# A fused attention and two-MLP kernel: its third layer by seven block products in place of eight

## The chip, the core and the metric

The kernel runs on one NeuronCore of one Trainium2 chip. The metric is device time in microseconds; less is better. The engines are named as the profile names them: TensorE (PE, and PEld for its weight loads), VectorE (DVE), ScalarE (ACT), GpSimd (POOL) and SyncE (SP), which here only issues DMAs.

## The reference, cut to what matters

```python
def reference(**kwargs):
    ...
    attn_out = _attn_ref(**attn_kwargs)          # 8 batches, 576 tokens each, 8 heads of 64
    x = attn_out.transpose(0, 2, 1, 3).reshape(B * S, H * D)      # 4608 x 512
    x = _moe_ref(x=x, **moe_kwargs)              # layers 1 and 2: max of three products, then w_out
    return _moe2_ref(x=x, **moe2_kwargs)

def _moe2_ref(x, w_in, w_out):                   # x 4608 x 512, w_in 512 x 2048, w_out 2048 x 512
    h = x @ w_in                                 # layer 3
    g = np.maximum(h, 0.0) + np.log1p(np.exp(-np.abs(h)))         # softplus
    return (g @ w_out).astype(np.float32)        # layer 4
```

Weights come as 64-bit floats, and the kernel narrows them itself.

## The kernel before, in words

The first part of the program goes over the eight batches. For each it computes attention and layers 1 and 2, and writes the result, transposed (512 features by 4608 tokens), to a DRAM tensor `x2d`. In this part the kernel also narrows `w_in` and `w_out` and writes them to the DRAM tensors `wi32` and `wo32` (`narrow_ahead`).

The second part computes layers 3 and 4. It goes over nine chunks `c` of 512 tokens and, in each, over sixteen blocks `f` of 128 of the 2048 hidden features. Every large product is made of three float32r matmuls: each operand is split into a high part and a low part (`split`: ScalarE copies the high part, VectorE subtracts it from the source to get the low one), and high times high, high times low and low times high are summed in PSUM.

`layer3(c, f)` issues 12 matmuls (four blocks of 128 input features, three terms each), all with a 128x128 stationary block of `w_in` and 512 moving columns, the tokens of the chunk. ScalarE then takes softplus from PSUM into `t`, and `split_g` splits it. `layer4(c, f, tt)` uses the split softplus as the stationary operand and 512 columns of `w_out` as the moving one; for one `f` it issues 12 matmuls, three for each of the four token blocks `tt`, and adds into one of four PSUM banks `acc`. The loop over `seq` issues `layer3` three steps ahead of `layer4`. The split `w_in` (`wi_parts`) stays in SBUF for the whole second part. The tokens of the next chunk are loaded and split during the current one (`load_x2`). After a chunk's last `f`, `store` copies the banks out and writes them with 32-row DMAs.

The last batch (`n + 1 == B`) has room for preparing the second part: in ten slots (six of layer 1, four of layer 2) the code loads `wi32` blocks and the first chunk of `x2d`, and splits them. Tile pools of that preparation lie where the attention's pools lay, so some loads wait for attention's last readers.

The order of instructions on each engine comes from a scheduler that keeps the order in which code is written, unless an instruction is free to go earlier; `tc.issue_after` pins work behind an instruction. SyncE issues nearly all DMAs in order: one that waits holds back all that are behind it. Its transfers also share one queue.

## Time and profile before

| | |
|---|---|
| median of three runs | 1338.63 us (1335.36 to 1340.78) |
| profiled execution, time | 1338.1 us |
| profiled execution, span from first to last instruction | 1336.1 us |
| TensorE busy (matmuls) | 1299.5 us, 97% of the span |
| VectorE busy | 539.5 us, 40% |
| ScalarE busy | 443.5 us, 33% |
| first matmul of layer 3 | 534.4 us from the span's start |
| last matmul of layer 4 | starts at 1331.6 us |

Busy times are sums over one profiled execution, and the two parts of the program differ: read each part by itself. A matmul's recorded duration contains the filling and emptying of the array and overlaps the next one's, so the cost of one in a stream is the interval between starts, not its duration.

### The profile page before, as it was taken

What the parts mean: (1) busy time and instruction counts of PE and PEld (TensorE: products, weight loads), DVE (VectorE), ACT (ScalarE), POOL (GpSimd) and SP (SyncE); (2) the same over time, 40 slices, a digit from 0 to 9 for tenths busy, and PEclk for the clock granted to TensorE, in tenths of its full rate; (3) what the DMA queues carried; (4) which work ended last, traced back from release to release, by engine and by line L of the source; (5) the groups of instructions that cost most, each with busy time, mean ns of one, the idle gap of its engine ahead of it and who ended that gap; (6) DMA issues with size and microseconds to landing.
All of it is one profiled execution on the core that took longest, in us unless ns stands there. A gap on an engine that the chain in (4) does not pass through costs nothing.

```text
span 1336.1 us, 20625 instructions
## 1 busy us (share of the span) xinstructions
PE 1299.5 (97%) x8656; PEld 1098.0 (82%) x8656; DVE 539.5 (40%) x904; ACT 443.5 (33%) x758; POOL 0.7 (0%) x6
## 2 busy tenths in 40 slices
PE   4879999999999999999999999999999999999998
PEld 3769898898988899888888888888888888888887
DVE  4787778786878746512111121121111211211111
ACT  3544434444343435623222222232222222322221
POOL 0000000000000000000000000000000000000000
PEclk9899999999999999999999999999999999999999
DMA  9883677877677407401002011010010110100101
GB/s 279 205 207 100 164 202 183 205 204 204 180 209 204 122 36 223 152 0 46 18 3 62 1 32 32 0 52 13 15 49 0 32 32 1 26 6 1 32 0 32
DMA packets 61853, 119.12 MB, mean 89 GB/s; under 512 B 11072, under 2 KB 28736, under 8 KB 61760
## 3 DMA queue, kind: packets, MB, share of 16 engines
q1 hardware_dynamic: 55984, 106.66, 29.8%
q10 hardware_dynamic: 5776, 11.14, 2.5%
q8 instruction: 68, 1.11, 0.4%
q14 instruction: 25, 0.20, 0.1%
HBM read 90.51 MB, written 27.26 MB: 88 GB/s over the span
## 4 chain that ended last, share of the span: by engine, by line
PE 92%; DVE 4%; DMA 2%; issue 1%; SPq 1%; ACT 1%; DVEq 0%
PE ps L396 58%; PE acc L766 10%; PE acc L767 10%; PE acc L765 10%; PE ps_w L375 2%; DMA wraw<-in_moe_w_dram 1%; PE ps_s L247 1%; PE ps_e L286 1%; PE ps_v L306 1%; DMA vt<-in_v_dram 1%; DVE pwlo L108 0%; DVE wraw L89 0%; PE ps_k L199 0%; DVE vT L223 0%; DVE wsb L97 0%
## 5 line engine op out<-in xcount | busy, mean ns | idle before, releaser
L108 DVE TENSOR_TENSOR glo<-t,ghi 128x512 fp32r<-128x512 f32 x144 | 99.7, 692 | 620.5 <-ACT ghi L107 620.5
L749 ACT ACTIVATE t<-ps 128x512 f32<-128x512 f32 x144 | 86.4, 600 | 546.7 <-PE ps L396 546.2
L396 PE MATMUL ps<-x2hi,wilo 128*128 128x512 f32 x576 | 228.0, 396 | 0.0
L396 PE MATMUL ps<-x2lo,wihi 128*128 128x512 f32 x576 | 227.0, 394 | 0.0
L396 PE MATMUL ps<-x2hi,wihi 128*128 128x512 f32 x576 | 226.7, 394 | 0.0
L767 PE MATMUL acc<-w2hi,glo 128*128 128x512 f32 x576 | 225.9, 392 | 0.0
L766 PE MATMUL acc<-w2lo,ghi 128*128 128x512 f32 x576 | 225.7, 392 | 0.0
L765 PE MATMUL acc<-w2hi,ghi 128*128 128x512 f32 x576 | 224.4, 390 | 0.0
L396 PE MATMUL ps<-a2hi,pwhi 128*128 128x288 f32 x576 | 129.5, 307 | 2.5 <-ACT a2hi L107 1.3
L396 PEld LDWEIGHTS ps<-x2lo,wihi 128*128 128x128 f32 x576 | 108.1, 188 | 25.8
L396 PEld LDWEIGHTS ps<-x2hi,wilo 128*128 128x128 f32 x576 | 108.3, 188 | 25.1
L766 PEld LDWEIGHTS acc<-w2lo,ghi 128*128 128x128 f32 x576 | 108.1, 188 | 25.0
L765 PEld LDWEIGHTS acc<-w2hi,ghi 128*128 128x128 f32 x576 | 108.2, 188 | 24.8
L396 PEld LDWEIGHTS ps<-x2hi,wihi 128*128 128x128 f32 x576 | 108.2, 188 | 24.6
L767 PEld LDWEIGHTS acc<-w2hi,glo 128*128 128x128 f32 x576 | 108.1, 188 | 23.1
L396 PE MATMUL ps<-a2lo,pwhi 128*128 128x288 f32 x576 | 124.6, 298 | 0.7 <-DVE a2lo L108 0.7
L396 PE MATMUL ps<-a2hi,pwlo 128*128 128x288 f32 x576 | 124.7, 299 | 0.0
L396 PEld LDWEIGHTS ps<-a2hi,pwhi 128*128 128x128 f32 x576 | 93.4, 192 | 15.8 <-ACT m L419 5.9
L396 PEld LDWEIGHTS ps<-a2lo,pwhi 128*128 128x128 f32 x576 | 94.0, 191 | 0.9 <-DVE a2lo L108 0.9
L396 PEld LDWEIGHTS ps<-a2hi,pwlo 128*128 128x128 f32 x576 | 94.0, 191 | 0.0
L107 ACT ACTIVATE ghi<-t 128x512 fp32r<-128x512 f32 x144 | 90.9, 631 | 4.2
L421 DVE TENSOR_TENSOR m<-ps,m 128x576 f32<-128x576 f32 x96 | 72.3, 753 | 30.6 <-PE ps L396 28.3
(85 smaller groups left out, 1300.4 us busy)
## 6 DMA issues: line engine op xcount, KB each, us to landing
qraw<-in_q_dram SPq DMA_DIRECT2D x112, 140.0 KB
kraw<-in_k_dram SPq DMA_DIRECT2D x96, 140.0 KB
wraw<-in_moe_w_dram SPq DMA_DIRECT2D x18, 512.0 KB
x2d<-xs ACTq DMA_DIRECT2D x32, 288.0 KB
x2r<-x2d SPq DMA_DIRECT2D x36, 256.0 KB
out_dram<-o SPq DMA_DIRECT2D x136, 64.0 KB
raw<-in_moe_w_in_dram SPq DMA_DIRECT2D x16, 512.0 KB
raw<-in_moe_w_out_dram SPq DMA_DIRECT2D x16, 512.0 KB
```

The source lines that it names most:

```text
L107: nc.scalar.activation(out=hi, in_=src, func=AF.Copy)
L108: nc.vector.tensor_tensor(out=lo, in0=src, in1=hi.bitcast(F32), op=ALU.subtract)
L247: nc.tensor.matmul(ps[G][cols, hh, :HS], w[rows, cols], x[rows, g, hh * HS : hh * HS + HS], start=True, stop=True,)
L286: nc.tensor.transpose(ps[: 32 * TI, i // hi, (i % hi) * P : (i % hi) * P + P], e[:, i], ident,)
L306: nc.tensor.matmul(ps[32 * g : 32 * g + 32, G, :D], t[:, i, 32 * g : 32 * g + 32], vt[n][:, NG * g + G, i, :], start=(i == 0), stop=(i == ...
L375: nc.tensor.matmul(ps[cols, G, : units * P].rearrange("p (w x) -> p w x", w=units), ppT[n][rows, cols], wsb[rows, 4 * c : 4 * c + units, g ...
L396: nc.tensor.matmul(o, w, xx, start=first, stop=last)
L421: nc.vector.tensor_tensor(out=m, in0=ps[:, :, :HS], in1=ms[n, f], op=ALU.max)
L749: nc.scalar.activation(out=t, in_=ps, func=AF.Softplus)
L765: nc.tensor.matmul(ps, ghi[:, cols], whi, start=(f == 0), stop=False)
L766: nc.tensor.matmul(ps, ghi[:, cols], wlo, start=False, stop=False)
L767: nc.tensor.matmul(ps, glo[:, cols], whi, start=False, stop=(f == F2 - 1))
```

## The change

Layer 3 is computed in units `(c, j)`, one for a pair of feature blocks `j` and `j + 8`. The weights of a pair are seen as 2x2 blocks (two halves of the 512 input features, two feature blocks), the tokens as 2x2 blocks (two halves of the input features, two halves of 256 tokens). One level of Strassen's scheme (Winograd's form) takes seven block products in place of eight; each is six matmuls of 256 columns (two blocks of 128 input features, three terms). It needs four sums of weight blocks, four sums of token blocks, and additions of the products, which VectorE makes (`sums`, and four additions in `layer3`). ScalarE copies the first product out of PSUM.

Weight sums are made once for a pair (`make_pair`), split, written to a DRAM tensor `wic` (14,336 bytes in each of 128 partitions, 1.835 MB a pair) and read back for every later chunk into a ring of two SBUF buffers (`get_pair`): pairs 2, 3, 0 and 1 are made in the last batch, 4 to 7 in chunk 0. `w_in` no longer stays in SBUF. The four PSUM banks of layer 3 are single-buffered (`l3`, tags l30 to l33). `layer4` takes a pair at once and runs one step behind. `wi32` is stored by pairs, in pieces of 512 bytes.

```diff
+    BATCH_END = {
+        0: [("load", 2)],
+        1: [("load", 3)],
+        2: [("make", 2), ("loadx", 0)],
+        4: [("make", 3), ("load", 0)],
+        5: [("load", 1)],
+        6: [("make", 0), ("makex", 0)],
+        7: [("makex", 1), ("makex", 2)],
+        8: [("makex", 3)],
+        9: [("make", 1), ("load", 4), ("load", 5)],
+    }
...
+                    def make_pair(j):
+
+                        u = wus.pop(j)
+                        sums(
+                            u,
+                            (
+                                (4, 0, 3, ALU.add),
+                                (5, 4, 1, ALU.subtract),
+                                (6, 1, 0, ALU.subtract),
+                                (7, 2, 5, ALU.subtract),
+                            ),
+                        )
+                        t = ring.tile([P, 2, 7, 2, P], F32R, tag="ring", name="wc")
+                        split(u[:, 1:8], t[:, 0], t[:, 1])
+                        nc.sync.dma_start(
+                            out=wic[j], in_=t.rearrange("p h a k x -> p (h a k x)").bitcast(F32)
+                        )
+                        pairs[j] = t
...
+    def product(out, w, x, wi, xi):
+        terms = [
+            (w[:, a, wi, k], x[b][:, xi, k]) for k in range(2) for a, b in ((0, 0), (0, 1), (1, 0))
+        ]
+        for i, (l, r) in enumerate(terms):
+            nc.tensor.matmul(out, l, r, start=(i == 0), stop=(i == len(terms) - 1))
+
+    def layer3(c, j):
...
+        w, x = pairs.pop(j), x2[c]
+        pa, pb, pc, pd = (
+            l3.tile([P, 2, HC], F32, tag=f"l3{i}", name=f"ps_3{i}") for i in range(4)
+        )
+        product(pa[:, 0], w, x, 0, 0)
+        product(pb[:, 0], w, x, 1, 1)
+        product(pb[:, 1], w, x, 4, 4)
+        product(pc[:, 0], w, x, 3, 3)
+        product(pc[:, 1], w, x, 5, 5)
+        product(pd[:, 0], w, x, 6, 2)
+        product(pd[:, 1], w, x, 2, 6)
+        h = cp.tile([P, 7, HC], F32, tag="h", name="h")
+        add = nc.vector.tensor_tensor
+        nc.scalar.activation(out=h[:, 3], in_=pa[:, 0], func=AF.Copy)
+        add(out=h[:, 0:5:4], in0=h[:, 3:4].to_broadcast([P, 2, HC]), in1=pb, op=ALU.add)
+        add(out=h[:, 5:7], in0=h[:, 4:5].to_broadcast([P, 2, HC]), in1=pc, op=ALU.add)
+        add(out=h[:, 3], in0=h[:, 6], in1=pc[:, 0], op=ALU.add)
+        add(out=h[:, 1:3], in0=h[:, 5:7], in1=pd, op=ALU.add)
+        done = last_of(mybir.EngineType.DVE)
+        g = h[:, 0:4].rearrange("p a t -> p (a t)")
+        nc.scalar.activation(out=g, in_=g, func=AF.Softplus)
+        hi = gp.tile([P, 2, CH], F32R, tag="ghi", name="ghi")
+        lo = gp.tile([P, 2, CH], F32R, tag="glo", name="glo")
+        split(g, hi.rearrange("p a t -> p (a t)"), lo.rearrange("p a t -> p (a t)"))
...
+    def get_pair(c, j):
+        if c == 0 and j >= 4:
+            make_pair(j)
+            return
+        pairs[j] = ring.tile([P, 2, 7, 2, P], F32R, tag="ring", name="wc")
+        nc.sync.dma_start(
+            out=pairs[j].rearrange("p h a k x -> p (h a k x)").bitcast(F32), in_=wic[j]
+        )
+
+    seq = [(c, j) for c in range(NCH) for j in range(FP)]
...
+    for i in range(len(seq) + 1):
         if i < len(seq):
...
+            c, j = seq[i]
+            with tc.issue_after(layer3(c, j)):
...
+                if i + 2 < len(seq):
+                    get_pair(*seq[i + 2])
...
+                if c + 1 < NCH:
+                    if j == 1:
+                        load_x2(c + 1)
+                    if 3 <= j < 7:
+                        make_x2(c + 1, j - 3, x2p0 if c % 2 else x2p1)
+        if i >= 1:
+            layer4(*seq[i - 1])
```

On TensorE, one unit of the second part of the program stood so before; `ps_7470` is the PSUM tile of `layer3(c, f)`, and the first of the matmuls of `layer4` follow:

```order
L396 MATMUL ps_7470<-x2hi,wihi 128x512
L396 MATMUL ps_7470<-x2lo,wihi 128x512
L396 MATMUL ps_7470<-x2hi,wilo 128x512
...
L765 MATMUL acc_6957<-w2hi,ghi 128x512
L766 MATMUL acc_6957<-w2lo,ghi 128x512
L767 MATMUL acc_6957<-w2hi,glo 128x512
```

In the changed program a unit of TensorE stands so; `wc` is the ring buffer with a pair's seven split weight blocks, and ps_7320 to ps_7323 are the banks pa, pb, pc and pd:

```order
L799 MATMUL ps_7320<-x2hi,wc 128x256
L799 MATMUL ps_7320<-x2lo,wc 128x256
L799 MATMUL ps_7320<-x2hi,wc 128x256 x2
...
L799 MATMUL ps_7321<-x2hi,wc 128x256
...
L799 MATMUL ps_7322<-x2hi,wc 128x256
...
L799 MATMUL ps_7323<-x2hi,wc 128x256
...
L845 MATMUL acc_6977<-w2hi,ghi 128x512
L846 MATMUL acc_6977<-w2lo,ghi 128x512
L847 MATMUL acc_6977<-w2hi,glo 128x512
```

Per two feature blocks, 24 matmuls of 512 columns have become 42 of 256 in layer 3, and the 24 of layer 4 follow as one group of 512 columns each, as before.

On SyncE's queue, from the last narrowed block of `w_out` to the end of the first loads of the second part, before (`wi_x` and `x2r` are loads for splitting, `w_x` is a block of `w_out`):

```order
L685 DMA wi_x<-wi_62 128x512 x4
L702 DMA x2r<-x2d 128x512
L685 DMA wi_x<-wi_62 128x512
...
L685 DMA wi_x<-wi_62 128x512 x3
L727 DMA w_x<-wo_63 128x512
L702 DMA x2r<-x2d 128x512
L727 DMA w_x<-wo_63 128x512 x3
```

The same place of SyncE in the changed program; `wu` is a pair's four weight blocks before the sums, `xu` the tokens before theirs, `wic<-wc` the write of a made pair and `wc<-wic` its reading back:

```order
L697 DMA wu<-wi_62 128x1024 x2
L720 DMA wic<-wc 128x3584
L728 DMA xu<-x2d 128x2x256 x4
L697 DMA wu<-wi_62 128x1024
L785 DMA w_x<-wo_64 128x512 x3
L720 DMA wic<-wc 128x3584
...
L728 DMA xu<-x2d 128x2x256
L720 DMA wic<-wc 128x3584
L697 DMA wu<-wi_62 128x1024
L785 DMA w_x<-wo_64 128x512 x2
L870 DMA wc<-wic 128x3584
```

The third and fourth writes (pairs 0 and 1) and two loads of `w_x`, which wait for VectorE's splits of earlier `w_out` blocks, now stand ahead of the first reading back, that of pair 2 for unit (0, 2).

On VectorE, inside chunk 0 where most is added (unit (0, 4), after the additions of unit (0, 3)), where there were only `w2lo` and `glo` of 512 columns before:

```order
L822 TENSOR_TENSOR h<-h,ps_7218 128x2x256
L823 TENSOR_TENSOR h<-h,ps_7219 128x512
L824 TENSOR_TENSOR h<-h,ps_7219 128x256
L825 TENSOR_TENSOR h<-h,ps_7220 128x512
L111 TENSOR_TENSOR w2lo<-w_x,w2hi 128x512 x2
L704 TENSOR_TENSOR wu<-wu 128x256 x3
L111 TENSOR_TENSOR x2lo<-xu,x2hi 128x1536
L111 TENSOR_TENSOR glo<-h,ghi 128x1024
L704 TENSOR_TENSOR wu<-wu 128x256
L822 TENSOR_TENSOR h<-h,ps_7321 128x2x256
L111 TENSOR_TENSOR wc<-wu,wc 128x1792
```

VectorE's work of a unit has grown from two subtractions to the four additions at the top, a subtraction twice as long, and, in chunk 0, the sums and splits of a later pair and of the next chunk's tokens.

## Rows read from the trace of the kernel before

**Rows 1.** The page: busy time of engines, TensorE's granted clock, the chain of waits.

```profile
PE 1299.5 (97%) x8656; PEld 1098.0 (82%) x8656; DVE 539.5 (40%) x904; ACT 443.5 (33%) x758; POOL 0.7 (0%) x6
...
PEclk9899999999999999999999999999999999999999
...
PE 92%; DVE 4%; DMA 2%; issue 1%; SPq 1%; ACT 1%; DVEq 0%
```

**Rows 2.** Waits, all engines, 534.3 to 1332 us: first two and last row.

```profile
engine line waited for: us in total, times, longest us
DVE glo L108 <- ACT ghi L107: 620.5, 132, 4.8
ACT t L749 <- PE ps L396: 546.2, 131, 4.3
...
ACT o L774 <- DMA out_dram<-o: 2.5, 1, 2.5
```

**Rows 3.** By instruction: count, duration min/median/max in ns, first and last start in us.

```profile
L396 PEld LDWEIGHTS ps<-x2hi,wihi x576: 187/188/188, 534.3 to 1320.0; 128*128 128x128 f32 x192
L396 PE MATMUL ps<-x2hi,wihi x576: 387/392/400, 534.4 to 1320.2; 128*128 128x512 f32 x192
...
L767 PE MATMUL acc<-w2hi,glo x576: 388/391/398, 545.8 to 1331.6; 128*128 128x512 f32 x192
```

**Rows 4.** Timeline of TensorE over layer 2 of the last batch: first and last.

```profile
515.20 0.43 PE L396 MATMUL ps<-hhi,wo_hi 128*128 128x288 f32 x2
...
534.13 0.43 PE L396 MATMUL ps<-hhi,wo_lo 128*128 128x288 f32 x2
534.40 0.39 PE L396 MATMUL ps<-x2hi,wihi 128*128 128x512 f32 x1
```

**Rows 5.** Timeline of weight loads and matmuls after an idle moment of the loads.

```profile
499.94 0.30 PEld L396 LDWEIGHTS ps<-a2hi,pwhi 128*128 128x128 f32 x2 [0.84 <-issue]
499.94 0.53 PE L396 MATMUL ps<-a2hi,pwhi 128*128 128x288 f32 x2
...
500.31 0.42 PE L396 MATMUL ps<-a2lo,pwhi 128*128 128x288 f32 x2
```

**Rows 6.** Groups by shape on VectorE and ScalarE: busy us, mean ns | idle before.

```profile
L108 DVE TENSOR_TENSOR glo<-t,ghi 128x512 fp32r<-128x512 f32 x144 | 99.7, 692 | 620.5 <-ACT ghi L107 620.5
L421 DVE TENSOR_TENSOR m<-ps,m 128x576 f32<-128x576 f32 x96 | 72.3, 753 | 30.6 <-PE ps L396 28.3 <-ACT m L419 0.7
L108 DVE TENSOR_TENSOR pwlo<-ps_w,pwhi 128x256 fp32r<-128x256 f32 x16 | 6.7, 422 | 5.4 <-ACT pwhi L107 5.4
L107 ACT ACTIVATE ghi<-t 128x512 fp32r<-128x512 f32 x144 | 90.9, 631 | 4.2
L107 ACT ACTIVATE pwhi<-ps_w 128x512 fp32r<-128x512 f32 x64 | 38.1, 596 | 39.7 <-PE ps_w L375 20.3 <-DVE pwlo L108 19.5
L107 ACT ACTIVATE pwhi<-ps_w 128x256 fp32r<-128x256 f32 x16 | 6.1, 383 | 5.3 <-DVE pwlo L108 3.6 <-PE ps_w L375 1.7
```

**Rows 7.** Windows: busy us of each engine (instructions), granted clock, DMA share, GB/s.

```profile
core 0: us, PE busy (x) PEld busy (x) DVE busy (x) ACT busy (x) POOL busy (x), PEclk, DMA share, GB/s
480.00:534.00 54.00, 54.00 (x439) 50.43 (x438) 30.76 (x46) 25.69 (x44) 0.00 (x0) 1.00 0.44 142
508.00:536.00 28.00, 28.00 (x207) 27.71 (x206) 17.70 (x29) 16.73 (x30) 0.00 (x0) 1.00 0.89 284
327.00:330.00 3.00, 3.00 (x24) 3.00 (x23) 1.62 (x3) 0.71 (x2) 0.00 (x0) 1.00 0.93 360
631.00:639.00 8.00, 8.00 (x36) 6.52 (x35) 1.63 (x3) 1.54 (x3) 0.00 (x0) 1.00 0.51 131
700.00:800.00 100.00, 100.00 (x435) 81.30 (x434) 18.36 (x27) 26.58 (x44) 0.00 (x0) 1.00 0.11 32
```

**Rows 8.** Timeline of the last batch: VectorE's last results of layer 1; SyncE's loads.

```profile
503.50 0.76 DVE L421 TENSOR_TENSOR m<-ps,m 128x576 f32<-128x576 f32 x1 [0.24 <-PE ps L396]
...
518.50 0.75 DVE L108 TENSOR_TENSOR hlo<-m,hhi 128x576 fp32r<-128x576 f32 x1
...
462.65 45.94 SPq L685 DMA_DIRECT2D wi_x<-wi  x4
508.63 0.43 SPq L702 DMA_DIRECT2D x2r<-x2d  x1
```

206 lines of the change are left out of this document (99 added, 107 removed).

## The prediction

> **What bounds the kernel now.** I read the page first. TensorE is busy for 97% of the span, at the full granted clock in nearly every slice, and the chain of waits lies on it for 92% [rows 1]. So I asked next whether it ever waits in the part that is changed: the list of waits from 534.3 us on has no TensorE row at all; VectorE and ScalarE wait for each other and for TensorE [rows 2]. From there on the kernel is a stream of matmuls and nothing else, and its time is their number times the interval between starts. The first starts at 534.4, the last at 1331.6 us [rows 3], with 9 x 16 x 24 = 3456 between them: 797.2 / 3455 = 230.7 ns for one of 512 columns. Layer 3 owns half of them, 1728 x 0.2307 = 398.7 us; layer 4's half is not touched. The other engines have room: in 700 to 800 us VectorE is busy for 18 and ScalarE for 27 of 100 us, and DMA moves 32 GB/s [rows 7].
>
> **What a matmul of 256 columns costs.** This is the term that decides, and the trace has no such float32r matmul. The nearest is layer 2, with 288 columns and the same 128x128 weights: from 515.20 to 534.40 us stand 144 of them (72 rows of two) [rows 4], 19.20 / 144 = 133.3 ns each. A line through (288, 133.3) and (512, 230.7) has a slope of 0.435 ns per column and gives 119.4 ns at 256. At 2.4 GHz a column is 0.417 ns, and the same step down from 288 gives 120.0. I take 120.
>
> The bounds: it can't be dearer than the wider one, 133.3. Below, the weight load may set a floor. Each matmul has its own load, which now has fewer columns to hide behind. A load's duration of 188 ns [rows 3] is already longer than the 133 ns interval, so durations don't tell. What tells is a start after an idle moment: two loads take 0.30 us together, so the second, 0.19 long, starts 0.11 after the first; the third matmul starts 0.37 after the first, and less 0.13 for the second's interval the first began streaming at about 0.11 too [rows 5]. So the load path takes about 0.11 us per load: 111 ns is my lower bound, and at 120 the loads just fit, with some 10 ns to spare against 22 in layer 2.
>
> Layer 3 then has 9 x 8 x 42 = 3024 matmuls: 3024 x 0.120 = 362.9 us for 398.7, a gain of 35.8. The ends of the price: 111 gives 335.7 (gain 63), 133.3 gives 403.1 (loss 4.4). The break-even is at 398.7 / 3024 = 131.8 ns.
>
> The Trainium skill (TensorE: Matmul & The Clock Gate, Back-to-back issue gap) gives a gap of N / 2.4 + 2.5 ns: 215.8 at 512 and 109.2 at 256. By it the gain would be 372.9 - 330.2 = 42.7 us. The trace disagrees by 15 ns at 512 columns [rows 3], so the rows' line stands.
>
> **What VectorE and ScalarE gain in work.** Prices go along lines through rows [rows 6]: a VectorE operation takes 422 ns for 256 columns and 692 for 512, so 1.06 ns per column more: 1.23 us for 1024, 1.77 for 1536, 2.04 for 1792. The rows with a PSUM source (422; 753 for 576) lie on the same line. ScalarE: 383 at 256 from PSUM, 631 at 512, 0.83 per column more: 1.06 us for 1024, 1.70 for 1792. A unit (c, j) costs VectorE 3 x 0.69 + 0.42 + 1.23 = 3.7 us and ScalarE 0.38 + 1.06 + 1.06 = 2.5, while TensorE takes 42 x 0.120 + 24 x 0.231 = 5.0 + 5.5 = 10.6 us. In chunk 0 VectorE also makes four pairs (4 x (4 x 0.42 + 2.04) = 14.9 us), splits 16 blocks of `w_out` (11) and makes the next tokens (4 x 0.69 + 1.77 + 2 x 1.23 = 7): 8 x 3.7 + 33 = 62 us of 85. Both are hidden under TensorE. If they weren't, this would be seen at two places. The four banks of layer 3 are single: unit j+1 writes `pa` again 5.5 us (the group of layer 4) after unit j's last matmul, and `pd` still later; VectorE's last addition ends 0.7 us after that matmul. Layer 4 of unit j needs the split softplus, 0.7 + 1.06 + 1.06 + 1.23 = 4.1 us after it, and comes 10.6 us after it. Only the very first pair of units has no group of layer 4 between; there products come 0.7 us apart and each bank has over 3 us. Nothing in the steady state waits.
>
> **What DMA gains.** One reading back is 1.835 MB. Its buffer comes free when unit j's layer 3 ends and must be full when that of j+2 starts, 5.5 + 5.0 + 5.5 = 16.1 us later. With the tokens (1.05 MB) and the output (1.05) a chunk moves 16.8 MB in 84.6 us, 198 GB/s for 32 now. The program has moved 284 GB/s over 28 us and 360 over 3 [rows 7]; at 284 a pair takes 6.5 us, plus about 2 until it is told, and a chunk's tokens or output ahead of it 3.7. It is hidden, with 4 us to spare. The `wi32` writes in 512-byte pieces lie in the first part, where other transfers surround them and each has a slot of some 6 us; I cost them at nothing.
>
> **What waits at the seam.** Here I expect the loss. In the last batch VectorE has 54 - 31 = 23 us free in 54 [rows 7] and does the making of four pairs and the first tokens (14.9 + 7) in place of 20 short splits (14). But two operations of 2.04 us and the sums now stand between the maxima and subtractions of layer 1, which TensorE waits for within 4 PSUM buffers (503.5 to 518.5 us [rows 8]): about 1 us late. Loading of tokens starts when attention's last reader frees the place, near 508 us, as now [rows 8]; behind it stand 0.5 MB for pair 0, then the write of pair 3 (1.8) and 0.5 for pair 1. By 300 GB/s pair 0 is ready near 533 and pair 1 between 537 and 542, where unit (0, 1) asks for it at 539.6 + 1: 1 us. Then the queue: pair 2, needed by unit (0, 2) at about 551, is read after pair 1's write (issued at 537 or later, 6.1 us), another pair's load (1.7), two blocks of `w_out` (1.7) and its own 6.1, plus 2: 554, so 3 us. Pair 3 follows inside its slack. For small waits in chunk 0, which moves some 22 MB in 85 us (262 GB/s), I add 1. Sum 6 us, between 1 and 14.
>
> **The sum**, against the profiled execution's own 1338.1 us (span 1336.1 and 2.0 around it): 1338.1 - 35.8 + 6 = 1308.3. The median of the runs is 0.5 above that execution: 1308.8. I say 1308.5.
>
> **Rivals.**
> - **The interval stays at 133 ns** (slower). A fixed cost per matmul and load, not the columns, sets layer 2's 133. For it: two points make a line but show no floor just below the lower one. Against it: the 0.11 us between loads where nothing else holds them [rows 5]. Price: 403.1 for 398.7, plus 6: 1348.5. It decides from 131.8 ns on.
> - **Loads and matmuls take turns** (slower). If the array did one at a time, 1296 more loads at 0.11 would be 143 us against 1728 x 64 columns x 0.417 = 46 saved, so about 1435. Against it: 512 columns and a load would take 213 + 110 = 323 ns, and the row has 230.7 [rows 3]. The Trainium skill (same page, The mechanism) says this of them: a weight load overlaps running matmuls only where their row groups differ, and here each uses all rows; the trace disagrees, so it keeps 1 in 100.
> - **The ring runs dry.** One stretch of output moved 131 GB/s [rows 7], though there the stores waited for their copies. The gain left is 30 us, 3.7 for each of the eight chunks that read back everything: it is gone below 16.8 / 88.3 = 190 GB/s. At 170 a chunk takes 99 us: +14 for each, about 1420.
> - **A longer seam.** If the reads of pairs 2 and 3 and the making of pair 1 line up behind VectorE and one another, with 200 GB/s, some 18 us are lost: 1321.
>
> **Chances.** Forecast, with seams of 1 to 14 us and 118 to 123 ns: 0.78. Longer seam (or 125 ns), still faster by over 0.5%: 0.09. 133 ns, or a gain eaten to within 0.5%, 1332 to 1345: 0.05 for the latter, 0.04 for 1345 and above by the first. Dry ring: 0.03. Taking turns: 0.01. Half a per cent, 6.7 us, is what a measurement of this kernel tells from nothing, its runs lying 5 us apart. Faster 0.87, same 0.05, slower 0.08. The range reaches from 118 ns with a seam of 1 (1297) to 125 ns (378 us, gain 20.7) with 5: 1298 to 1323.
>
> **What would show it.** Layer 3's matmuls should start 120 ns apart; no wait of TensorE for VectorE, ScalarE or DMA after unit (0, 3), so that a chunk takes 84.6 us for 88.6; before that, waits for `wc` of a few us in all; DMA near 200 GB/s. The forecast is wrong if the interval is above 130, or if each unit begins with a wait for `wc`.

## The result and the profile after

The changed kernel takes 1296.75 us (median of four runs, 1292.94 to 1297.29), the kernel before 1337.55 in the same comparison (1335.36 to 1340.78): a ratio of 0.9687, 95% interval 0.9659 to 0.9715. It is faster by 3.1%. The prediction said 1308.5 us, between 1298 and 1323: right in direction and mechanism, and 1.25 us below the low end of its range. The profiled execution after took 1296.47 us, with a span of 1294.7.

The page of the changed kernel, the lines that answer to [rows 1]:

```profile
PE 1255.4 (97%) x9952; PEld 1131.4 (87%) x9952; DVE 754.2 (58%) x1171; ACT 459.4 (35%) x669; POOL 0.7 (0%) x6
...
PEclk9899999999999999999999999999999999999999
...
PE 91%; DMA 4%; DVE 3%; issue 1%; ACT 1%; SPq 0%; DVEq 0%
```

TensorE still is what the program runs on; VectorE has 215 us more work than before and ScalarE 16, and their shares of the chain have not grown. The waits of TensorE from the first matmul of layer 3 to the end, the whole list:

```profile
engine line waited for: us in total, times, longest us
PE ps L799 <- DMA wc<-wic: 0.9, 1, 0.9
PE ps L799 <- ACT xs L456: 0.7, 1, 0.7
```

In 754 us TensorE waits twice: once at its first unit, for ScalarE's last copy of layer 2 out of PSUM (`xs`), and once for the reading back of pair 2. So the second part is again a stream of matmuls without gaps, and what changed is their number and their interval. By instruction, as in [rows 3]:

```profile
L799 PEld LDWEIGHTS ps<-x2hi,wc x2016: 186/189/192, 536.5 to 1279.2; 128*128 128x128 f32 x184
L799 PE MATMUL ps<-x2hi,wc x2016: 277/282/386, 536.5 to 1279.3; 128*128 128x256 f32 x184
...
L847 PE MATMUL acc<-w2hi,glo x576: 388/389/442, 547.8 to 1290.2; 128*128 128x512 f32 x192
```

The stage, from the first start to the last, has shrunk from 797.2 to 753.7 us. To split it between the layers, the starts where the streams alternate are enough. In the kernel before, TensorE's timeline of one odd chunk and then of one even chunk; between a row and the next lie 12 matmuls (the rows between are left out):

```profile
850.06 0.40 PE L765 MATMUL acc<-w2hi,ghi 128*128 128x512 f32 x1
...
852.79 0.39 PE L396 MATMUL ps<-x2hi,wihi 128*128 128x512 f32 x1
...
855.60 0.40 PE L765 MATMUL acc<-w2hi,ghi 128*128 128x512 f32 x1
...
941.43 0.40 PE L396 MATMUL ps<-x2hi,wihi 128*128 128x512 f32 x1
...
944.21 0.39 PE L765 MATMUL acc<-w2hi,ghi 128*128 128x512 f32 x1
...
946.97 0.40 PE L396 MATMUL ps<-x2hi,wihi 128*128 128x512 f32 x1
```

In the odd chunk layer 4 took 2.73 us (227.5 ns a matmul) and layer 3 2.81 (234.2); in the even one layer 3 took 2.78 (231.7) and layer 4 2.76 (230.0). The two layers were never equal, and the chunks come in two kinds (the tokens of even chunks lie in one buffer, `x2p0`, those of odd chunks in another, `x2p1`). The same timeline of the changed kernel, odd chunk and even chunk, with 42 matmuls of layer 3 and 24 of layer 4 between the rows:

```profile
856.17 0.28 PE L799 MATMUL ps<-x2hi,wc 128*128 128x256 f32 x1
...
861.10 0.40 PE L845 MATMUL acc<-w2hi,ghi 128*128 128x512 f32 x1
...
866.55 0.28 PE L799 MATMUL ps<-x2hi,wc 128*128 128x256 f32 x1
...
898.09 0.28 PE L799 MATMUL ps<-x2hi,wc 128*128 128x256 f32 x1
...
903.12 0.39 PE L845 MATMUL acc<-w2hi,ghi 128*128 128x512 f32 x1
...
908.60 0.28 PE L799 MATMUL ps<-x2hi,wc 128*128 128x256 f32 x1
```

Odd: 4.93 us / 42 = 117.4 ns and 5.45 / 24 = 227.1. Even: 5.03 / 42 = 119.8 and 5.48 / 24 = 228.3. Over all starts of the two traces (means of the differences between neighbouring starts, by layer and chunk):

```
ns per matmul      layer 3: even chunks  odd    mean    layer 4: even  odd    mean
before                      231.3        234.0  232.5            229.7  228.2  229.0
after                       119.8        117.4  118.7            228.3  227.2  227.8
```

With these the time is accounted for, against the prediction's own sum:

| term | predicted | measured |
|---|---|---|
| layer 3, before | 1728 x 230.7 ns = 398.7 us | 1728 x 232.5 = 401.7 us |
| layer 3, after | 3024 x 120 = 362.9 us | 3024 x 118.7 = 359.0 us |
| layer 4 | not touched | 1728 x 229.0 = 395.7, now x 227.8 = 393.7 us |
| seam: first start of layer 3 | part of 6 us | 536.45 for 534.40: 2.05 us |
| seam: waits inside the stage | part of 6 us | 1.25 us |
| sum | -35.8 + 6 = -29.8 us | -42.7 - 2.0 + 2.05 + 1.25 = -41.4 us |

The rest came out as priced. VectorE's and ScalarE's operations have the durations that the lines through [rows 6] gave (688 ns for an addition of 512 columns, 1223 for the subtraction of 1024 and 1060 for the softplus of 1024), and the steady state stands so, in the columns of [rows 7] and beside its last line:

```profile
700.00:800.00 100.00, 100.00 (x639) 91.02 (x638) 44.33 (x60) 28.41 (x36) 0.00 (x0) 1.00 0.55 195
```

VectorE 44 of 100 us, ScalarE 28, DMA 195 GB/s: the forecast was 198.

At the seam SyncE's queue stands as the prediction read it from the order, but it runs earlier:

```profile
535.38 0.32 SPq L720 DMA_DIRECT2D wic<-wc  x1
535.75 1.31 SPq L697 DMA_DIRECT2D wu<-wi  x1
543.10 1.02 SPq L785 DMA_DIRECT2D w_x<-wo  x2
544.21 0.38 SPq L870 DMA_DIRECT2D wc<-wic  x1
```

The write of pair 1 is issued at 535.4 us (forecast: 537 or later), nothing waits for pair 1, and the reading back of pair 2 is issued at 544.2 behind two loads of `w_out` that waited for buffers. TensorE then waits 0.9 us for it, where 3 were forecast.

### The profile page after: what moved, and what is told of

Read it like the earlier page. It is cut to its first block, busy times and chain, and to the rows that moved or that the text cites. A ratio compares the mean times of both kernels' runs of the same rounds, so it can differ in the third digit from the quotient of the medians.

```text
span 1294.7 us, 23533 instructions
## 1 busy us (share of the span) xinstructions
PE 1255.4 (97%) x9952; PEld 1131.4 (87%) x9952; DVE 754.2 (58%) x1171; ACT 459.4 (35%) x669; POOL 0.7 (0%) x6
## 4 chain that ended last, share of the span: by engine, by line
PE 91%; DMA 4%; DVE 3%; issue 1%; ACT 1%; SPq 0%; DVEq 0%
PE ps L399 28%; PE ps L799 27%; PE acc L847 10%; PE acc L846 10%; PE acc L845 10%; PE ps_w L378 2%; DMA wraw<-in_moe_w_dram 1%; PE ps_v L309 1%; PE ps_s L250 1%; PE ps_e L289 1%; DMA wc<-wic 1%; DMA kraw<-in_k_dram 1%; DMA vt<-in_v_dram 1%; DVE pwlo L111 0%; DVE wraw L92 0%
## 5 line engine op out<-in xcount | busy, mean ns | idle before, releaser
L799 PE MATMUL ps<-x2hi,wc 128*128 128x256 f32 x2016 | 370.7, 282 | 1.6 <-DMA wc<-wic 0.9
L799 PEld LDWEIGHTS ps<-x2hi,wc 128*128 128x128 f32 x2016 | 316.1, 190 | 5.0 <-DMA wc<-wic 1.3
L799 PE MATMUL ps<-x2lo,wc 128*128 128x256 f32 x1008 | 283.7, 281 | 0.0
L799 PEld LDWEIGHTS ps<-x2lo,wc 128*128 128x128 f32 x1008 | 191.3, 190 | 2.8
L822 DVE TENSOR_TENSOR h<-h,ps 128x512 f32<-128x512 f32 x72 | 49.5, 688 | 228.3 <-PE ps L799 224.7
L828 ACT ACTIVATE h<-h 128x1024 f32<-128x1024 f32 x72 | 76.3, 1060 | 286.4 <-DVE h L825 286.4
L111 DVE TENSOR_TENSOR glo<-h,ghi 128x1024 fp32r<-128x1024 f32 x72 | 88.1, 1223 | 84.5 <-ACT ghi L110 84.5
L821 ACT ACTIVATE h<-ps 128x256 f32<-128x256 f32 x72 | 27.6, 384 | 188.1 <-PE ps L799 188.1
L399 PE MATMUL ps<-hhi,wo_hi 128*128 128x288 f32 x384 | 82.9, 298 | 0.0
```

What stands on the lines that cost most here:

```text
L111: nc.vector.tensor_tensor(out=lo, in0=src, in1=hi.bitcast(F32), op=ALU.subtract)
L399: nc.tensor.matmul(o, w, xx, start=first, stop=last)
L799: nc.tensor.matmul(out, l, r, start=(i == 0), stop=(i == len(terms) - 1))
L821: nc.scalar.activation(out=h[:, 3], in_=pa[:, 0], func=AF.Copy)
L822: add(out=h[:, 0:5:4], in0=h[:, 3:4].to_broadcast([P, 2, HC]), in1=pb, op=ALU.add)
L828: nc.scalar.activation(out=g, in_=g, func=AF.Softplus)
```

## The experiments

Two questions were open: whether everything that was costed at nothing really is hidden, and where the 11.6 us beyond the forecast come from. Where no number of runs is given, a run was executed once. The first part alone varies by more than 4 us between executions (see e8), so the readings go by the stage (from layer 3's first start to layer 4's last) and by the intervals.

**e1: an eighth product.** Every unit computes its first product twice (the repeat goes into the free half of its bank, and nothing reads it), 48 matmuls of 256 columns for 42. The number of columns is then that of the kernel before.

```diff
         product(pa[:, 0], w, x, 0, 0)
+        product(pa[:, 1], w, x, 0, 0)
```

> The changed kernel with one more block product per unit, whose result nobody reads (a repeat of the first, into the free half of its bank): 8 x 6 matmuls of 256 columns, 48 for 42. If the gain is the number of matmuls times an interval that the columns set, and everything else is hidden, 432 more at 118.7 ns add 51.3 us to the changed kernel's span of 1294.7: 1346, and the interval stays. If VectorE or DMA held units back anywhere, the added matmuls would fill waits and cost less.

It took 1347.08 us (before, on the same chip, 1339.23), and the stage became 50.9 us longer than that of the changed kernel; 432 more matmuls x 118.7 ns are 51.3, the wait for pair 2, worth 1.0 us of the stage, is gone, and layer 4's interval rose from 227.8 to 228.3 ns, 0.8 us. Layer 3's is unchanged (118.7). So the gain is set by the number of matmuls times their interval, and nothing beside TensorE sets the pace. Eight narrow products would have been slower than the kernel before.

**e2: longer groups in the kernel before.** Two feature blocks of layer 3, then two of layer 4: groups of 24 matmuls in place of 12, all of 512 columns.

```diff
-    SKEW = 3
-    END = 2
+    units = [seq[i : i + 2] for i in range(0, len(seq), 2)]
...
+        for c, f in units[i] if i < len(units) else ():
```

> The kernel before, with the layers' steps taken for two feature blocks at a time: 24 matmuls of layer 3, then 24 of layer 4, in place of 12 and 12; the same matmuls in all. Theory of group length (each change from one layer's stream to the other leaves about eleven longer intervals): layer 4's mean interval falls from 229.2 to about 227.8 ns and layer 3's from 232.4 to about 229.5, span 1336.1 to about 1329. Theory of place (where operands lie in SBUF sets the interval): both intervals stay within 0.5 ns, span 1336 +- 1.

1334.54 us (eight runs) for 1339.23, ratio 0.9966 (0.9955 to 0.9976); the stage is 793.4 us for 797.2. Layer 4's interval fell from 229.0 to 228.1 ns and layer 3's from 232.5 to 231.2, all of it in the even chunks (231.3 to 229.0; the odd ones stay at 234, so layer 3 fell by less than half of what was expected). So the grouping alone, which the change brought along, is worth 3.8 us of matmul intervals.

**e3: shorter groups in the changed kernel.** Each unit is cut in two: part of layer 3, half of layer 4's group, the rest of layer 3, the other half.

```diff
+        if middle:
+            layer4(*middle, (0, 1))
...
-            layer4(*seq[i - 1])
+            layer4(*seq[i - 1], (2, 3) if i < len(seq) else (0, 1, 2, 3))
```

> The changed kernel with each unit cut in two: four block products, half of layer 4's group, three products, the other half. The same matmuls, twice the changes between the streams. Theory of group length: layer 4's mean interval rises from 227.8 to about 229.3 ns (+2.6 us), layer 3's little, span about 1297.5. Theory of place: layer 4 stays at 227.8, span 1294.7 +- 0.7.

1297.46 us; the stage is 756.9 us for 753.7. One cut unit of an even chunk, and its first half:

```profile
885.58 0.28 PE L799 MATMUL ps<-x2hi,wc 128*128 128x256 f32 x1
...
888.45 0.39 PE L847 MATMUL acc<-w2hi,ghi 128*128 128x512 f32 x1
...
891.21 0.28 PE L799 MATMUL ps<-x2hi,wc 128*128 128x256 f32 x1
```

24 of layer 3 at 119.6 ns, then 12 of layer 4 in 2.76 us, 230.0 each. Over the whole stage layer 4 rose from 227.8 to 230.1 ns and layer 3 stayed at 118.6. Layer 4 went both ways as the theory says, but the length of its groups is not all. In even chunks of the changed kernel a group of layer 4 begins with nine intervals of 224 to 236 ns (231 in the mean) and then stays at 226 to 227; a group of 12 ends three matmuls later. In odd chunks of the same trace only the first interval is long (235). e3's half groups begin with nine such intervals in even chunks, and with nine or five in odd ones, where there was one. So e3 raised the number of beginnings and, in odd chunks, also what each of them costs. The beginnings of all kinds are set side by side under e17.

**e4: a pad of 32 bytes,** so that the ring of weights and the tokens of even chunks begin at multiples of 64 bytes, as those of odd chunks do. It was meant for the two kinds of chunk.

```diff
+    ctx.enter_context(tc.tile_pool(name="pad", bufs=1, side="right")).tile([P, 8], F32, name="pad")
```

> The changed kernel with 32 bytes of unused SBUF ahead of the pools on the right side, so that the ring and the first token buffer start at multiples of 64 bytes instead of 32 past one. In the changed kernel chunks with an even number (tokens in that buffer) show 120 ns per matmul of 256 columns, odd ones (tokens in a buffer at a multiple of 64) 117.4. Theory of place: even chunks fall to 117.4 or below, 5 x 336 x 2.6 ns = 4.4 us, span at most 1290.5; more if the weights' place counts too, since the ring is moved for all chunks. Theory that the parity has another cause (which of the two buffers, the chunk's other work): even chunks stay at 120, span 1294.7 +- 0.7.

1298.58 us, ratio 0.9694 (0.9675 to 0.9712). Even chunks stay at 119.7 ns, odd ones go from 117.4 to 117.8. The theory, as it was put, falls. This run also shows a dearer wait for pair 2, with the granted clock behind it; the timeline, and the window behind it (granted clock: third value from the end):

```profile
552.42 0.58 PE L800 MATMUL ps<-x2hi,wc 128*128 128x256 f32 x1 [2.11 <-DMA wc<-wic]
```

```profile
552.80:555.70 2.90, 2.90 (x15) 2.90 (x15) 0.00 (x0) 1.53 (x3) 0.00 (x0) 0.50 0.92 376
```

After 2.1 us without a matmul the granted clock is 0.50, the lower level of 1.2 GHz, for the next 2.9 us, and matmuls start 213 ns apart: the fifteen matmuls behind the wait cost 1.4 us more than at the upper level. In the changed kernel, after 0.9 us, it stayed at 1.00.

**e5: fewer columns in layer 3.**

```diff
+            n = HC if i == 0 else HC // 2
+            nc.tensor.matmul(out[:, :n], l, r[:, :n], start=(i == 0), stop=(i == len(terms) - 1))
```

> The changed kernel, but in layer 3 only the first of the six matmuls of a product has 256 columns, the other five have 128: 64 x 128 columns less per term, so part of the products is left out. It measures what sets the interval of layer 3's matmuls below 256 columns. Theory: the path of the weight loads takes about 0.11 us for each, which the prediction read from two loads after an idle moment; then the 2520 narrow matmuls start 108 to 111 ns apart instead of 118.7, and the stage gets 20 to 27 us shorter (run near 1273). Rival: nothing but columns counts (0.435 ns each): 63 ns, the stage 140 us shorter unless the DMA's 1.835 MB a unit, then at about 240 GB/s, end it earlier.

The kernel leaves out part of the products. 1291.0 us, where 1273 was expected. One unit, layer 4's group and layer 3's:

```profile
885.44 0.44 PE L846 MATMUL acc<-w2hi,ghi 128*128 128x512 f32 x1
...
890.99 0.28 PE L800 MATMUL ps<-x2hi,wc 128*128 128x256 f32 x1
...
895.67 0.44 PE L846 MATMUL acc<-w2hi,ghi 128*128 128x512 f32 x1
```

4.68 us / 42 = 111.4 ns: with 42% of the columns gone the interval fell by 7 ns of 119. So there is a floor of some 111 to 112 ns, where the prediction had its lower bound of 111. That it is the path of the weight loads is argued from [rows 5] (0.11 us between two loads); this run would look the same if another cost of a load and its matmul set it. Layer 3 gave back 21.7 us over the stage, as expected, but layer 4 took 5.1 back (its interval rose to 230.8 ns, the first of a group to 282), and some 10 us went into waits and the lower clock behind them, between 590 and 630 us (chunk 0 and its end), where VectorE and ScalarE, with the units shorter, came late. The matmuls of 256 columns run 5 to 8% above the floor; fewer columns would gain almost nothing.

**e6: no reading back** from chunk 1 on: two pairs of weights serve all later units, so the result is another one.

```diff
+        if c:
+            pairs[j] = made[j % 2]
+            return
```

> The changed kernel without the reading back from chunk 1 on: pairs 6 and 7 as made in chunk 0 stay in the ring and serve every later unit, so the weights of chunks 1 to 8 are those of two pairs only. It takes away 117 MB of transfers and every dependence on them. Theory: the reading back is hidden and costs TensorE nothing, so the stage stays within 1 us of 753.7 us and both intervals stay (118.7 and 227.8 ns). Rival: the transfers take something from the reads of weights and tokens in SBUF and stretch the intervals; then these fall by a nanosecond or more, 3 to 6 us in all.

1297.15 us. The window (columns again as in [rows 7]) shows the DMA gone, 22 GB/s for 197, and the same number of matmuls in it as in the changed kernel (1897 there, give or take what the record misses):

```profile
900.00:1200.00 300.00, 300.00 (x1900) 272.42 (x1899) 136.43 (x179) 87.03 (x104) 0.00 (x0) 1.00 0.08 22
```

Both mean intervals agree with the changed kernel's to 0.02 ns, and the stage is 752.6 us: 1.1 less, the wait for pair 2. The reading back is hidden, and transfers don't touch the intervals.

**e7: two further reads a unit,** meant to find where the ring runs dry.

```diff
+        for r in range(2 if c else 0):
+            x = wup.tile([P, 8, 2, P], F32, tag="wu", name="wx")
+            nc.sync.dma_start(out=x.rearrange("p a k x -> p (a k x)"), in_=wic[j, :, 0:2048])
```

> The changed kernel with two further reads of 1.05 MB behind each reading back from chunk 1 on, into the two buffers that the making of pairs has left free: a unit then moves 4.2 MB in place of 2.1, which at 10.45 us would be 400 GB/s. It measures where the ring runs dry. Theory: transfers are hidden up to what DMA can move, and the most that the trace of the kernel before has shown is 360 GB/s; a unit then takes 11.6 us or more and TensorE waits for wc in each: at least 70 us more in all, near 1370, and near 1570 if only 284 GB/s can be held. Rival: reading goes on at over 400 GB/s, and the time stays near 1297.

1463.19 us, between the two prices, but it did not measure what it was for. The list of TensorE's waits names the ring for 3.8 us only:

```profile
PE acc L845 <- ACT ghi L110: 108.8, 53, 3.0
...
PE ps L799 <- DMA wc<-wic: 3.8, 4, 1.7
```

The scheduler, with the added reads in the queue, put matmuls of layer 4 (17 of 24 for the unit at 907 us) right behind the same unit's layer 3, where they wait for softplus and split; the waits are those of another order. What it does show: in slices of the page DMA moved up to 421 GB/s, over the 360 of [rows 7]. At which load the ring runs dry stays open.

**e8: the additions twice.**

```diff
-        add = nc.vector.tensor_tensor
+        def add(**kw):
+            for r in range(2):
+                nc.vector.tensor_tensor(**kw)
```

> The changed kernel with each of the four additions of the products made twice, 2.5 us more of VectorE in each unit of 10.45 us (3 x 0.69 + 0.42); the result is the same. Theory: VectorE has the room (44 of 100 us busy in the steady state, 59 of 84 in chunk 0), and the four single banks come free in time, so the steady state stays as it is and the time is within 2 us of 1297; in chunk 0 VectorE then has 79 of 84 us and a wait of a few us may show there. Rival: the chain from the last product over additions, softplus and split to layer 4, or the bank that the next unit writes, has no room: then a wait of up to 2.5 us shows in each of 72 units, up to 180 us.

1293.7 us. VectorE is busy for 198 of 300 us in place of 137, and TensorE has the same stream; chunk 0, with 75 of 80 us, brought one wait of 0.5 us for `glo`:

```profile
900.00:1200.00 300.00, 300.00 (x1894) 272.15 (x1893) 198.35 (x292) 87.73 (x104) 0.00 (x0) 1.00 0.56 199
540.00:620.00 80.00, 79.51 (x503) 71.83 (x502) 74.59 (x116) 37.86 (x46) 0.00 (x0) 1.00 0.72 266
```

The stage is 753.6 us for the changed kernel's 753.7. The single banks and VectorE have 2.5 us a unit to spare. This run also tells how the first part varies: it is the same program there, and layer 3 began at 533.6 us, in e6 at 538.2.

**e9 and e10: places.** The ring and the tokens of even chunks exchanged; the tokens of odd chunks moved up by 102,400 bytes.

```diff
-                    ring = ctx.enter_context(
...
                     x2p0 = ctx.enter_context(
...
+                    ring = ctx.enter_context(
```

> The changed kernel with the places of two pools in SBUF exchanged, which are equally large: the tokens of even chunks (x2p0) lie where the ring of weights lay, and the ring where they lay. Layer 3's interval is 119.8 ns in even chunks, 117.4 in odd ones, whose tokens lie elsewhere. Theory: where the moving tokens lie, in relation to the weights, sets it; then the even chunks' 119.8 changes by a nanosecond or more, and the odd ones' 117.4 may, since the ring has moved for them too. Rival: the place has no part in it, and both stay to the tenth.

```diff
-    x2p1 = ctx.enter_context(tc.tile_pool(name="x2p1", bufs=1, reuse_waits="tile"))
...
     w32p = ctx.enter_context(tc.tile_pool(name="w32p", bufs=3, reuse_waits="tile"))
+    x2p1 = ctx.enter_context(tc.tile_pool(name="x2p1", bufs=1, reuse_waits="tile"))
```

> The changed kernel with the tokens of odd chunks (x2p1) moved in SBUF from below to above the buffers of layer 4's operands; nothing else of layer 3 moves, the buffers of layer 4's operands move by the tokens' size. Theory of the place: the odd chunks' 117.4 ns changes by half a nanosecond or more, the even ones' 119.8 stays. Rival: both stay to the tenth.

1293.69 and 1295.74 us (before: 1335.12), and 119.8 and 117.4 ns in both, to the tenth. I took the place for excluded. But both moves were multiples of 4096 bytes.

**e11: reading back first.**

```diff
+                if i < 2:
+                    get_pair(*seq[i + 2])
                 if c == 0:
                     for f in (j, j + FP):
...
-                if i + 2 < len(seq):
+                if 2 <= i < len(seq) - 2:
```

> The changed kernel with the reading back of pairs 2 and 3 issued ahead of the next blocks of w_out, whose loads wait for buffers. Theory: the wait of 0.9 us for wc in unit (0, 2) comes from the reading back standing behind those loads on SyncE's queue; it goes, the stage is 1 us shorter than 753.7 us, and no other wait takes its place. Rival: the reading back waits for the ring's buffer or shares its bandwidth with the write of pair 1, and the wait stays; or the blocks of w_out now come late, and layer 4 of unit (0, 1) or (0, 2) waits.

1297.07 us in one run, with layer 3 beginning at 538.2 us; the stage is 752.6 us, 1.1 shorter, and the wait for `wc` is gone without another in its place. One run would not show this, since the wait was missing from e3 and e8 too, which kept the old order; but it is missing from all seven traces with the new order. e12 to e16 and e18 keep this edit.

**e12: the same remainder for all tokens.**

```diff
+    ctx.enter_context(tc.tile_pool(name="pad", bufs=1, side="right")).tile([P, 88], F32, name="pad")
```

> The reading back issued first, as in the run before this, and a pad of 352 bytes at the start of SBUF's upper side, so that the tokens of even chunks begin at the same remainder of 4096 bytes as those of odd chunks (3712). The exchange and the move of places shifted tokens by multiples of 4096 bytes (7 and 25 of them) and kept this remainder, and the pad of 32 bytes did not bring it together; so they did not exclude it. Theory of the remainder: even chunks take the odd ones' 117.4 ns, the stage is 1680 x 2.4 ns = 4 us shorter than 752.6 us, and the ratio to the kernel before falls to about 0.965. Rival: even chunks stay near 119.8, and the place in SBUF has no part in it; then the ratio is 0.968.

1297.07 us (five runs), ratio 0.9688 (0.9675 to 0.9702). The two kinds of chunk are gone, but the other way round: all nine take 119.8 ns. Two units, of the neighbouring chunks 3 and 4:

```profile
802.57 0.28 PE L800 MATMUL ps<-x2hi,wc 128*128 128x256 f32 x1
...
807.60 0.40 PE L846 MATMUL acc<-w2hi,ghi 128*128 128x512 f32 x1
...
886.57 0.28 PE L800 MATMUL ps<-x2hi,wc 128*128 128x256 f32 x1
...
891.60 0.40 PE L846 MATMUL acc<-w2hi,ghi 128*128 128x512 f32 x1
```

5.03 us in both. The pad had moved the ring as well. In every run so far with 256 columns, chunks whose tokens begin at the same remainder of 512 bytes as the weights have 119.6 to 119.8 ns, and the others 117.4 to 117.8. So the distance counts, not the place.

**e13: the tokens of all chunks apart from the weights** (a pad between the two pools).

```diff
+                    ctx.enter_context(tc.tile_pool(name="pad0", bufs=1, side="right")).tile(
+                        [P, 88], F32, name="pad0"
+                    )
                     x2p0 = ctx.enter_context(
```

> The reading back issued first, and a pad of 352 bytes between the ring of weights and the tokens of even chunks. In units of 512 bytes the tokens of even chunks then begin 160 bytes behind the weights, as those of odd chunks do in the changed kernel; the weights stay where they were. Theory of the distance (what counts is the remainder of the tokens against that of the weights; 0 gives 119.8 ns, 160 gives 117.4): all chunks take 117.4, layer 3 takes 355 us for 359, the stage 748.5 us, and the ratio to the kernel before is near 0.9655. Rival, the remainder of the tokens alone (3712 of 4096 goes with whatever the odd chunk has): already contradicted by the last run, where it gave 119.8; if it came out so again, nothing is gained.

1289.59 us (five runs, 1286.12 to 1291.9; before 1338.8), ratio 0.9629 (0.9605 to 0.9653): faster than both kernels, 0.6% under the changed one by the ratios. The same two places:

```profile
802.94 0.28 PE L802 MATMUL ps<-x2hi,wc 128*128 128x256 f32 x1
...
807.87 0.40 PE L848 MATMUL acc<-w2hi,ghi 128*128 128x512 f32 x1
...
885.98 0.28 PE L802 MATMUL ps<-x2hi,wc 128*128 128x256 f32 x1
...
890.91 0.40 PE L848 MATMUL acc<-w2hi,ghi 128*128 128x512 f32 x1
```

4.93 us in both, 117.4 ns, and layer 4 falls with it to 227.2 (227.1 in all chunks but the first). The stage is 747.4 us, 5.2 less than in e11: 1680 x 2.4 ns = 4.0 us from layer 3 and 1.2 from layer 4.

**e14 to e16: other distances.** The same pad with other sizes, one for even and one for odd chunks (a second pad ahead of `x2p1`); of e14:

```diff
+                    ctx.enter_context(tc.tile_pool(name="pad0", bufs=1, side="right")).tile(
+                        [P, 120], F32, name="pad0"
+                    )
...
-    op = ctx.enter_context(tc.tile_pool(name="op", bufs=3, reuse_waits="tile"))
+    op = ctx.enter_context(tc.tile_pool(name="op", bufs=2, reuse_waits="tile"))
+    ctx.enter_context(tc.tile_pool(name="pad1", bufs=1)).tile([P, 104], F32, name="pad1")
```

> The same with other distances, 32 bytes for the tokens of even chunks and 64 for those of odd ones, and two buffers for the output's copies in place of three to make room. If only equality counts, both give near 117.4 ns. If the distance counts by steps of 64 bytes, 64 gives 119.8 and 32 gives 117.4. Anything between says that the interval follows the distance gradually.

> The same with 128 bytes for even chunks and 256 for odd ones. If only equality (in units of 512 bytes or more) counts, both give near 117.4 ns; if in units of 128 or 256, one or both give 119.8.

> The same with 96 bytes for even chunks and 352 for odd ones: two more points. If 96 and 352 differ, then a distance of 256 does not bring the pattern back; if one of them is under 117.4 ns, there is more to be had than the 4 us.

The three took 1292.82, 1299.93 and 1302.2 us. With the runs before, the interval of layer 3 by the distance of tokens from weights (start of the tokens less start of the weights in SBUF, as a remainder of 512 bytes; all blocks inside them begin at multiples of 512):

```
bytes                     0      32     64     96     128    160    192    256    352
ns (256 columns)          119.8  116.8  117.7  119.9  119.9  117.4  117.8  120.0  119.9
the same modulo 128       0      32     64     96     0      32     64     0      96
```

Neither equality alone nor steps of 64 bytes: the pattern repeats every 128 bytes to within a nanosecond, with two good distances (32 and 64) and two bad ones (0 and 96). Of the distances tried, the best is half a per cent of the interval under 117.4.

**e17: the kernel before, with its tokens moved.**

```diff
+                    ctx.enter_context(tc.tile_pool(name="pad0", bufs=1, side="right")).tile(
+                        [P, 16], F32, name="pad0"
+                    )
...
+    ctx.enter_context(tc.tile_pool(name="pad1", bufs=1)).tile([P, 24], F32, name="pad1")
```

> The kernel before, whose layer 3 has matmuls of 512 columns, with two pads: the tokens of odd chunks, which lay 32 bytes from the weights (in units of 128 bytes) and had 234.0 ns, are brought to a distance of 0; those of even chunks, which lay at 0 and had 231.5, to 64. Theory of the distance, in units of 128 bytes: the odd chunks take 231.5 ns, and the even ones change. Rival, that at 512 columns the two kinds have another cause: the odd chunks stay at 234.0.

1333.0 us, for 1340.32 on the same chip; the stage is 791.1 us for 797.2. An odd chunk and an even one:

```profile
802.46 0.39 PE L396 MATMUL ps<-x2hi,wihi 128*128 128x512 f32 x1
...
805.18 0.39 PE L769 MATMUL acc<-w2hi,ghi 128*128 128x512 f32 x1
...
807.90 0.39 PE L396 MATMUL ps<-x2hi,wihi 128*128 128x512 f32 x1
...
884.16 0.39 PE L396 MATMUL ps<-x2hi,wihi 128*128 128x512 f32 x1
...
886.96 0.39 PE L769 MATMUL acc<-w2hi,ghi 128*128 128x512 f32 x1
```

Odd chunks fell from 234.0 to 226.7 ns, and even ones, brought to 64, rose from 231.3 to 233.3. So the places of operands made the two kinds there too. That it was the tokens' place alone is not shown: the second pad moves layer 4's operands along with the tokens of odd chunks, and they too then begin at the weights' remainder.

Distance 0 gave 231.3 in the kernel before and 226.7 here. The means hide why; the intervals one by one do not (the first twelve of a group, medians over chunks 1 to 7; in brackets the distance of the moving operand from the stationary one, which in layer 4 is that of `w_out` from the split softplus):

```
ns from one start to the next
before, layer 3, even chunks (0)              236 233 236 224 231 236 228 233 231 227 227 237
before, layer 3, odd chunks (32)              231 232 237 237 231 234 235 233 232 237 237 231
before, layer 4, even chunks (0)              229 233 236 224 231 236 228 232 231 227 227 228
before, layer 4, odd chunks (0)               232 231 227 227 227 227 227 227 227 227 226 228
changed, layer 4, even chunks (0)             229 233 236 224 231 236 228 233 231 227 227 227
changed, layer 4, odd chunks (0)              235 227 227 227 227 227 227 227 227 227 227 227
e17, layer 3, even chunks (64)                233 233 233 233 233 233 233 233 233 233 233 233
e17, layer 4, even chunks (0)                 226 236 228 232 231 227 227 227 227 227 227 227
e17, layers 3 and 4, odd chunks (0 and 0)     227 227 227 227 227 227 227 227 227 227 227 227
```

At distance 0 every group of either layer comes to 227 ns. What differs is how many other intervals it begins with, from none to nine, for the most part one series that is entered at different points (it ends 236, 228, 232, 231). At 32 and 64 the interval stays at 231 to 237 throughout. So groups of 12 cost nothing extra where they begin without long intervals, and nearly all of e2's gain comes from even chunks, where they begin with nine.

**e18: layer 4's operands apart.**

```diff
+    ctx.enter_context(tc.tile_pool(name="pad4", bufs=1)).tile([P, 16], F32, name="pad4")
     cp = ctx.enter_context(tc.tile_pool(name="cp", bufs=2, reuse_waits="tile"))
```

> The version with the tokens apart from the weights by 32 bytes (in units of 128) in all chunks, here by a pad of 96 bytes in place of 352, and in layer 4 a pad of 64 bytes between the split softplus (stationary) and w_out (moving), which lay at distance 0. If units of 128 bytes are right, layer 3 keeps 117.4 ns in all chunks. Layer 4's 227.1 ns then changes if its matmuls follow the same rule as layer 3's; at 512 columns the kernel before had its lower interval at distance 0, so I expect no gain, 227 to 230 ns.

The tokens of even chunks stay apart from the weights here too, by a pad of 96 bytes in place of e13's 352. 1299.31 us. Layer 4 rose from 227.2 to 231.3 ns, +7.1 us; layer 3 stayed below 119 in all chunks but went from 117.4 to 118.0, in odd chunks too, whose tokens had not moved. So layer 4 follows the places as well, at 512 columns with 0 better than 64. That layer 3 moved too suggests that one stream's places reach a little into the other's interval.

## Why the prediction came out too high

Its mechanism holds at each step. Layer 3's 3024 matmuls start 118.7 ns apart for a forecast of 120; VectorE, ScalarE and the reading back are hidden (e6, e8); DMA moves 195 GB/s for 198; TensorE doesn't wait after unit (0, 2), and a chunk takes 83.6 us for 84.6. None of the rivals came: the interval did not stay at 133 ns, loads and matmuls did not take turns, the ring did not run dry, and the seam was shorter, not longer. Where the ring would have run dry, e7 failed to show.

The 11.6 us beyond the forecast are three terms: 5.0 from the shares of the two layers, 3.9 from layer 3's interval, 2.7 from the seam. With any one of them as forecast the time would lie inside the range. The range itself begins above its own lower corner, which the prediction works out as 1297 and states as 1298.

**The step that failed** is "Layer 3 owns half of them, 1728 x 0.2307 = 398.7 us; layer 4's half is not touched". One mean over the stage stood for two streams. Layer 3 was the slower of them and owned 401.7 us, and layer 4 was touched: 395.7 became 393.7. These 5.0 us are the largest of the three terms and the only one without a bound in the prediction, and without them its own arithmetic, with the measured interval and seam, gives 1338.1 - (398.7 - 359.0) + 3.3 = 1301.7, inside the range. Layer 4's part is shown in the main. Where the change is described, layer 4's group stands "as before"; its columns do, but the group grew from 12 matmuls to 24. e2, which changes the groups alone, brought 229.0 to 228.1 in the kernel before, of the 227.8 after. The rest lies in odd chunks, where a group begins with one long interval in place of two; what sets that number is not shown. That layer 3 was dearer than layer 4 came in good part from where operands lie in SBUF: e17 took 7 ns from its odd chunks (tokens and layer 4's operands moved together). In even chunks its groups begin with nine long intervals, as layer 4's do.

**Mis-sized terms.** The price of 120 ns was within 1.1% in the mean, 3.9 us. It is the price of even chunks (119.8), and the odd ones are cheaper, by the distance of their tokens from the weights (e12, e13); a line through two rows could not hold that. e5's floor, 111.4 ns, agrees with the prediction's lower bound of 111. (The working of that bound says to take one interval of 0.13 us from 0.37; it takes two to reach the 0.11 that it states.) The seam was put at 6 us and cost 3.3: of the late start of 2.05 us, 0.7 is the wait for `xs`, which was not foreseen, and most of the rest is within what the first part varies from run to run (533.6 to 538.2 us in the runs of e6 and e8, the same program there). Pair 1 was ready in time for a forecast of 1 us late, and pair 2 was 0.9 us late for 3.

The pages. The Trainium skill (TensorE: Matmul & The Clock Gate, LDWEIGHTS (loading the stationary operand)) prices a load at its columns / 1.2, 106.7 ns for 128; e5's 111.4 is near it and, as a floor, agrees. The isolated gap by the Trainium skill (same page, Back-to-back issue gap), 109.2 ns at 256 columns, is below every interval measured here (116.8 to 120.0). The gain of 42.7 us that the prediction worked out from it is just what layer 3 gained (401.7 - 359.0), but by luck: its gaps are 16.7 ns too low at 512 columns and 9.5 at 256, which is 28.9 us over 1728 matmuls and 28.7 over 3024, and the two cancel. The Trainium skill (SBUF — State Buffer, Who interferes with whom) gives TensorE two independent read ports, one for the moving operand and one for weight loads; e12, e13 and e18 don't fit two reads without any effect on each other: a shift of the two operands against each other by 32 to 64 bytes (in units of 128) changes the interval by about 2%. On which path they meet no run here shows.

**What stays open:** the rule behind the places. It repeats every 128 bytes at 256 columns, prefers 0 at 512, and neighbouring streams count. Open too is what sets the number of long intervals at the beginning of a group, which differs with the places of both streams (e17) and with where the group before was cut (e3).

## What to carry to other kernels

Where one engine is a stream without waits, price each of its streams from its own starts, by stage and by kind, and ask of each what the change does to its grouping; a mean over the stage hid 5 us here. Look at the intervals one by one before you take a mean for a speed. When equal work has two speeds that alternate with a buffer, look at where in SBUF the buffers begin: a pad of 352 bytes took 5.2 us off the stage here, 0.4% of the kernel's time. A test that moves a buffer must change its remainder, or it excludes nothing.

## What the runs showed of the hardware

- Start of operands in SBUF: moving operand against stationary weights, at float32r and 256 columns, 116.8 to 118.0 ns at distances of 32 and 64 bytes modulo 128, 119.6 to 120.0 at 0 and 96. At 512 columns the interval settles at 226 to 227 ns at distance 0 (both layers, before, changed and e17); its mean is 234.0 at 32 (before, odd chunks), and 233.3 (e17) and 231.3 (e18) at 64.
- A group of matmuls of 512 columns that follows another stream begins with none to nine intervals of 224 to 237 ns before it settles at 226 to 227, by the places of the operands and by where the group before ended (before, changed, e3, e17).
- Pairs of a weight load of 128x128 and a matmul in float32r come no closer than 111.4 ns on average (e5, with 5 of 6 matmuls at 128 columns), with loads of 189 ns on record.
- At the granted clock of 0.50, the level of 1.2 GHz, matmuls start 213 ns (256 columns, e4) and 427 ns (512 columns, e7) apart, which is their columns divided by 1.2; at the level of 2.4 GHz the same division gives 106.7 and 213.3, and the intervals are 10 to 13 and 13 to 21 ns above it.
